# Windowed attention with sink tokens, then a gated two-layer MLP, on one core: a searched order of work written out, with another load order and another first score stage

## The chip, the core and the metric

The kernel runs on one core of one Trainium2 chip. The metric is device microseconds (us) per execution. One launch takes the inputs from HBM and leaves the output in HBM.

The engines are TensorE (PE: matmuls and transposes), VectorE (DVE), ScalarE (ACT: exp, tanh, copies), GpSimd (POOL) and SyncE (SP: issues most DMAs). DMAs can also be issued by ACT and by POOL; each issuing engine has a queue of its own.

## The reference

```python
# q, k, v: (4 batches, 8 heads, 768 positions, 64)
scores = q @ k.T / 8                        # per batch and head
keep = (key < 4) | (0 <= query - key < 128) # 4 sink keys, window of 128
a = softmax(where(keep, scores, -1e9))
x = (a @ v) as (4*768 tokens, 8*64 features)
h = x @ w_in                                # 512 -> 2048
out = (h * sigmoid(beta * h)) @ w_out       # 2048 -> 512
```

## The kernel before, in words

**Tiling.** The 3072 tokens are cut into 8 half batches (hb 0 to 7) of 384 tokens. A *unit* u is a pair of heads in one half batch, so there are 32 units, four to a half batch. PE does six kinds of step, and their names are used in this document:

- T(u): transposes q and k of a unit on PE (line 725, six matmuls), then two copies PSUM to SBUF (`qkT`). From half batch 3 on, DMA transposes do this instead.
- S(n): a *burst* of score tiles, matmuls of 64 rows (line 823). ACT takes the exp of each tile into a slot of `E` (line 840), and DVE or POOL multiply the masks in (lines 848, 854, 858). A tile is 128x1024: four 128x128 blocks of two heads each; `s` blocks touch the sinks, `d` blocks the diagonal, `p` blocks the block left of it.
- F: sink scores of a half batch against the four sink keys (line 870), exp into `ES` (line 874).
- A(u): attention times values (lines 915 and 926), then on DVE a reciprocal (line 930) and a product into `onorm` (line 932).
- R(u): transposes `onorm` on PE (line 952) and copies it into `xT`; from half batch 3 on by DMA.
- H(T, m): one of 16 column blocks of the first MLP layer for half batch T: four matmuls (line 970), tanh on ACT (line 975), product on DVE into `g` (line 977).
- O(T, t, j): four of the 16 matmuls of an output tile (line 993); the last is followed by a copy to `osb` and a store.

H and O carry most of PE's work: 128 H and 100 O.

**Order.** Nothing is ordered at run time. A planner in the kernel's own Python (class Graph) gives each operation an estimated duration. PE's steps of the first part are written by hand (the string in line 1188 and the list `early` in line 1228); later ones are taken by the loop in line 1260, which asks of each kind when it could start (`head`). `arrange` then re-sorts all engines with one constant for a hand-over between engines (HOP, line 35) and may move a PE step past up to ten others (WIDE, SKIP). PSUM has eight banks; `choose` picks the one free first. `any_of` lets several engines compete for a copy, a cast or a mask. While PE would wait in the first part, the planner inserts matmuls on a tile of ones (line 1212, "fill").

**Loads.** Before: SP issues q of half batch 0 in four pieces of 192 KB, its v in three pieces of 256 KB (rows of 256 B), q and k of half batch 1 (768 KB each), beta, then the weight pieces w0 to w15 (512 KB each; line 616). ACT issues the four pieces of k of half batch 0. Weights go through six staging buffers; w6 waits until w0 is cast, and so on. Values of the sink tokens (`vS`) for batch 0 come from a matmul with a selection matrix (`first_values_pe`, line 676): PE line 680, then DVE line 682.

Of the kernel before, what the change touches and what calls it, by code (L numbers as in the profile page):

```python
# [7 lines left out]
ALU = mybir.AluOpType  # L8
# [14 lines left out]
class Op:  # L23
    __slots__ = ("eng", "fn", "deps", "signal", "count", "waits", "sem", "vc", "dma", "seq", "end", "ns", "alts",
                 "group", "tail", "hold", "lock", "chain", "preds", "ready", "left", "succ", "at")


class Graph:
# [6 lines left out]
    HOP = 180  # L35
    SKIP = 3
    PAD = 100
    STRICT = 1
    WIDE, EARLY = 10, 60000
    SLACK = 0  # L40
# [3 lines left out]
    def __init__(self):  # L44
        self.ops = []
        self.writers = {}
        self.readers = {}
        self.last_x = {}
        self.free = {e: 800.0 for e in self.ENGINES}
        self.dma_free = 2500.0  # L50
        self.stalls = [(16000.0, 1100.0), (34000.0, 700.0)]
        self.port = {"gp": 0.0, "dve": 0.0}
        self.group = 0
        self.filler, self.fill_to = None, 0

# [4 lines left out]
    def add(self, eng, fn, ns=0, r=(), w=(), x=(), dma=None, alts=None, after=(), hold=550, chain=None, lock=False):  # L60
# [9 lines left out]
        o.lock = lock  # L70
# [22 lines left out]
        for p, _ in deps:  # L93
            at = max(at, p.end + (0 if p.eng == eng and not p.dma else self.HOP))
# [4 lines left out]
    def fill(self, fn, r):  # L99

        def one():
            o = Op()
            wide = self.free["pe"] + 2 * self.filler[0] <= self.fill_by
            o.eng, o.fn, o.dma, o.ns = "pe", fn[wide], None, self.filler[0] * (1 + wide)
            o.signal, o.count, o.waits, o.vc, o.lock = False, 0, [], None, False
            o.deps = [(p, True) for k in r for p in self.writers[k]]
            return o
        self.filler, self.fill_to = (self.COLD, one), self.group

    def shut(self, o, eng):  # L110

        return self.port["gp" if eng == "dve" else "dve"] if eng == "gp" or eng == "dve" and o.lock else 0.0

    def place(self, o, at):
# [3 lines left out]
        if o.dma:  # L118
# [4 lines left out]
            o.end = self.dma_free + 1000  # L123
        else:
            o.end = self.free[o.eng] = at + o.ns

    def at(self, keys):

        t = 0.0
        for k in keys:  # L130
            ws = self.writers.get(k)
            if not ws:
                return None
            t = max([t] + [p.end + self.HOP for p in ws])
        return t

    def bank_at(self, k):
        return max([0.0] + [p.end + self.HOP for p in self.last_x.get(k, ())])

    def arrange(self):  # L140
# [10 lines left out]
        follow, last = {}, None  # L151
        for o in ops:
            if o.chain is not None:
                if last is not None:
                    follow[id(last)] = o
                    o.left += 1
                last = o
        after = None
        for o in reversed(ops):
            o.tail = max([s.tail + self.HOP for s in o.succ] + [0.0])  # L160
# [3 lines left out]
            o.tail += o.ns + (2000 if o.dma else 0)  # L164
        groups = {}
        for o in ops:
            if o.eng == "pe":
                groups.setdefault(o.group, []).append(o)
        todo_pe = list(groups.values())
        self.free = {e: 800.0 for e in self.ENGINES}  # L170
        self.dma_free = 2500.0
        self.stalls = [(16000.0, 1100.0), (34000.0, 700.0)]
        self.port = {"gp": 0.0, "dve": 0.0}
        new, planned = [], set()

        def ready(o, e):
            return max([0.0] + [p.end + (0 if p.eng == e and not p.dma else self.HOP) for p in o.preds])

        def done(o):
            planned.add(id(o))  # L180
            new.append(o)
            for s in o.succ:
                s.left -= 1
                if s.left == 0 and s.eng != "pe":
                    pool.append(s)
            if id(o) in follow:
                s = follow[id(o)]
                s.left -= 1
                if s.left == 0:
                    pool.append(s)  # L190

        pool = [o for o in ops if o.left == 0 and o.eng != "pe"]
        while todo_pe or pool:
            best = None
            wide = self.SKIP if self.free["pe"] > self.EARLY else self.WIDE
            if todo_pe and todo_pe[0][0].group <= self.fill_to:
                wide = self.STRICT
            for i, grp in enumerate(todo_pe[:wide]):
                own = set(map(id, grp))
                if any(id(p) not in planned and id(p) not in own for o in grp for p in o.preds):  # L200
                    continue
                t, off = self.free["pe"], 0.0
                for o in grp:
                    t = max([t] + [p.end + self.HOP - off for p in o.preds if id(p) not in own and p.eng != "pe"])
                    off += o.ns
                if best is None or t < best[0] - self.SLACK:
                    best = (t, "pe", i)
                if t <= self.free["pe"]:
                    break
            by_eng = {}  # L210
            for o in pool:
                opts = []
                for e, (fn, ns) in o.alts.items():
                    t = max(self.free[e], ready(o, e), self.shut(o, e))
                    if o.dma:
                        t = max(t, self.dma_free - 3000)
                    opts.append((t + ns, t, e))
                _, t, e = min(opts)
                by_eng.setdefault(e, []).append((t, o))
            first = {}  # L220
            for e, c in by_eng.items():
                t0 = min(c, key=lambda x: x[0])[0]
                first[e] = (t0, max((x for x in c if x[0] <= t0), key=lambda x: x[1].tail)[1])
# [4 lines left out]
            for e, (t0, o) in first.items():  # L228
# [4 lines left out]
            if e == "pe":  # L233
                grp = todo_pe.pop(what)
                late = t + self.PAD if t > self.free["pe"] + 40 else t
                self.fill_by = late
                while self.filler and grp[0].group <= self.fill_to and self.free["pe"] + self.filler[0] <= late:
                    o = self.filler[1]()
                    self.place(o, max([self.free["pe"]] + [p.end + self.HOP for p, _ in o.deps]))
# [5 lines left out]
                for o in grp:  # L245
                    self.place(o, max([self.free["pe"]] + [p.end + self.HOP for p in o.preds if p.eng != "pe"]))
# [149 lines left out]
def _program(nc, G, sb, ps, q, k, v, w_in, w_out, beta, out):  # L396
# [4 lines left out]
    CUT = 3  # L401
# [25 lines left out]
    sel = sb("sel", (128, 128), BF16)  # L427
# [16 lines left out]
    WIDE_W, SPL, BQ = 2, ('act','gp'), "sp"  # L444
    EARLY, BST, SOON = 0, [1,2,2]+[3]*5, 2200
    LANES, QUADS = [6,7], [5,7]
    P = ps("P", (128, 8, 512))

    def add(eng, fn, ns, r=(), w=(), x=(), dma=None, after=(), hold=550, chain=None):
        return G.add(eng, fn, ns, r, w, x, dma, None, after, hold, chain)  # L450

    def any_of(alts, r=(), w=(), x=(), lock=False):

        return G.add(min(alts, key=lambda e: G.free[e] + alts[e][1]), None, 0, r, w, x, None, alts, lock=lock)
# [22 lines left out]
    held, reserve = {7}, [False]  # L477
    ring, two = [[6,5,4]], [[0,1],[2,3],[0,1],[2,3],[4,5]]

    def choose(n):  # L480

        if n == 1:
            runs = [[j] for j in (LANES if reserve[0] else range(8)) if j not in held]
            return min([(max(G.bank_at(("B", j)) for j in c), c[0] not in LANES, c) for c in runs], default=None)
        runs = [[]]
        for _ in range(n // 2):
            runs = [r + [i, i + 1] for r in runs for i in range(r[-1] + 1 if r else 0, 7, 2) if not held & {i, i + 1}]
        return min([(max(G.bank_at(("B", j)) for j in c), c[0] in LANES, c) for c in runs], default=None)

    def banks_at(n, more=False):  # L490
        c = choose(n)
        if c and more:
            rest = [G.bank_at(("B", j)) for j in range(8) if j not in held and j not in c[2]]
            return max(c[0], min(rest)) if rest else None
        return c and c[0]

    forced = []

    def take(n):
        if forced:  # L500
            got = [forced.pop(0) for _ in range(n)]
        elif ring[0]:
            if n == 1:
                got = ring[0].pop(0)
                ring[0].append(got)
                got = [got]
            else:
                got = list(range(n))
                if n == 2:
                    got = two.pop(0)  # L510
        else:
            got = choose(n)[2]
# [20 lines left out]
    def consts():  # L533
# [5 lines left out]
        add("gp", lambda e: e.memset(sel[:, :], 0.0), 80, w=["sel0"])  # L539
        add("gp", lambda e: e.tensor_copy(  # L540
            sel[:, :].rearrange("p (h w) -> p h w", w=16)[:, :, 0:NSINK],
            ident[:, 0:NSINK].unsqueeze(1).to_broadcast([128, H, NSINK])), 150, r=["sel0", "ident"], w=["sel"])
# [47 lines left out]
    def load(hb, n, i):  # L590

        b, t0, z = hb // 2, hb % 2 * HALF, hb % NSTG
        if n == "v" or hb >= CUT:
            src = {"q": q, "k": k, "v": v}[n][b, :, t0 + i * 128:t0 + (i + 1) * 128, :].rearrange("h p d -> p h d")
            dst, keys, ns = stg[n][z][:, i, :, :], [("stb", n, z, i)], NV0 if hb < 2 else 1092
        else:
# [4 lines left out]
            ns = NQ0 * len(keys) if hb == 0 else 1950 if hb == 1 else 2080  # L601
            keys = [("stg", n, z, j) for j in keys]
        after = [("stg", n, z, j) for j in range(4)] if hb in range(CUT, CUT + NSTG) and n != "v" else ()
        add("act" if hb == 0 and n == "k" and Q2 else "sp", lambda e: e.dma_start(dst, src), ns, w=keys,
            dma=f"d{n}{z}{'' if i is None else i}", after=after, chain=hb if hb < 3 else None)

    def load_w(j):
# [721 lines left out]
```

## Time and profile before

| what | value |
|---|---|
| three timed runs | 221.11, 222.12, 222.97 us (median 222.12) |
| profiled execution: its own time, first to last instruction | 219.7 us |
| median of the runs less that span | 2.4 us |
| PE busy | 213.4 us, 97% |
| PE weight loads | 120.8 us, 55% |
| DVE / ACT / POOL busy | 138.1 / 147.2 / 75.2 us |
| granted TensorE clock, mean | 1.000 |
| fill matmuls on ones | 35, 11.3 us busy |
| moved by DMA | 39.86 MB |

The profiled execution is one execution apart from the timed runs. A busy engine is not one that advances the result: fill counts as busy. The chain of work that ended last is 38% line 993 and 36% line 970, both on PE.

### The profile page before, as it was taken

To read this page: it belongs to the slowest core of one execution; us is meant where nothing else is said; L and a number is where in the kernel's file an instruction comes from. 1 tells how busy PE (TensorE), PEld (TensorE's weight loads), DVE (VectorE), ACT (ScalarE), POOL (GpSimd) and SP (SyncE) were. 2 spreads that over 40 slices of the span, in tenths; PEclk is the share of its full clock that TensorE was granted. 3 is DMA by queue.
4 is the path that set the end of the run, shared out by engine and by line. 5 is a ranking of instruction groups with operands and counts; after the bars stand their busy time and mean duration, and the time that the engine had idled before them with its cause. 6 is when DMAs were issued, how large, how long until landed. Compare 5 with 4: busy or idle time off the path is not lost.

```text
span 219.7 us, 4563 instructions
## 1 busy us (share of the span) xinstructions
PE 213.4 (97%) x1776; PEld 120.8 (55%) x1793; DVE 138.1 (63%) x293; ACT 147.2 (67%) x241; POOL 75.2 (34%) x140
## 2 busy tenths in 40 slices
PE   8999999999999999999999999999999999999995
PEld 3455557555575575446554556446565456465443
DVE  1697899697774278358960788478886248088000
ACT  2698999586975798459865597275886574187211
POOL 7344551112550790067103770184101770100100
PEclk9999999999999999999999999999999999999999
DMA  6999999999989998499837997659949111400122
GB/s 190 240 302 364 357 287 357 371 298 204 226 185 188 225 141 217 92 253 218 196 74 180 228 182 203 139 142 237 136 98 209 40 63 27 144 2 0 51 95 95
DMA packets 94717, 39.86 MB, mean 181 GB/s; under 512 B 82072, under 2 KB 89512, under 8 KB 94696
## 3 DMA queue, kind: packets, MB, share of 16 engines
q1 hardware_dynamic: 91928, 33.28, 68.9%
q0 software_dynamic: 1680, 5.51, 7.5%
q10 hardware_dynamic: 1088, 0.79, 1.1%
q8 instruction: 14, 0.23, 0.5%
q14 instruction: 7, 0.06, 0.1%
HBM read 27.37 MB, written 6.29 MB: 153 GB/s over the span
## 4 chain that ended last, share of the span: by engine, by line
PE 88%; DVE 6%; DMA 3%; ACT 2%; issue 1%; ACTq 0%
PE P L993 38%; PE P L970 36%; PE P L926 5%; PE P L823 4%; DMA k_stage<-in_k_dram 3%; DVE E L858 2%; PE P L725 2%; PE P L952 1%; DVE g L977 1%; PE P L915 1%; DVE E L848 1%; PE P L870 1%; PE P L1212 1%; DVE w_in L528 1%; ACT E L840 0%
## 5 line engine op out<-in xcount | busy, mean ns | idle before, releaser
L970 PE MATMUL P<-xT,w_in 128*128 128x384 bf16 x512 | 86.8, 327 | 0.4 <-ACT w_in L523 0.2
L993 PE MATMUL P<-w_out,g 128*128 128x512 bf16 (+2 forms) x383 | 84.6, 371 | 1.0 <-issue 0.2
L975 ACT ACTIVATE t<-P,hbeta 128x384 f32<-128x384 f32 x128 | 72.4, 590 | 17.6 <-PE P L970 11.0
L977 DVE SCALAR_TENSOR_TENSOR g<-t,P 128x384 bf16<-128x384 f32 x128 | 67.9, 550 | 21.1 <-ACT t L975 15.7
L970 PEld LDWEIGHTS P<-xT,w_in 128*128 128x128 bf16 x512 | 49.0, 98 | 33.4 <-DVE g L977 0.8
L993 PEld LDWEIGHTS P<-w_out,g 128*128 128x128 bf16 x400 | 37.3, 98 | 40.5 <-issue 0.5
L840 ACT ACTIVATE E<-P 128x1024 bf16<-128x1024 f32 x44 | 43.1, 1036 | 14.1 <-PE P L823 14.1
L854 POOL TENSOR_SCALAR_AFFINE_SELECT E<-E 128x512 bf16<-128x512 bf16 x59 | 38.8, 684 | 27.4 <-ACT E L840 27.2
L1011 POOL DMA_DIRECT2D out_dram<-osb x21 | 11.8, 562 | 63.5 <-ACT osb L523 63.5
L523 ACT ACTIVATE osb<-P 128x512 f32<-128x512 f32 x14 | 8.4, 597 | 25.1 <-PE P L993 25.0
L932 DVE TENSOR_TENSOR onorm<-P,rden 128x384 bf16<-128x384 f32 x32 | 17.6, 554 | 0.8
L529 DVE TENSOR_SCALAR osb<-P 128x512 f32<-128x512 f32 x9 | 6.2, 688 | 15.0 <-PE P L993 14.9
L848 DVE TENSOR_TENSOR E<-E,maskS 128x512 bf16<-128x512 bf16 x16 | 8.8, 564 | 10.4 <-ACT E L840 10.4
L926 PE MATMUL P<-vaug,E 128*128 128x65 bf16 x352 | 15.0, 193 | 0.0
L926 PEld LDWEIGHTS P<-vaug,E 128*128 128x128 bf16 x352 | 14.0, 97 | 1.4 <-ACT E L840 0.4
L823 PEld LDWEIGHTS P<-qkT 64*128 64x128 bf16 x288 | 9.5, 94 | 7.6 <-issue 4.3
L823 PE MATMUL P<-qkT 64*128 64x128 bf16 (+1 forms) x288 | 13.2, 230 | 0.1
L1212 PE MATMUL P<-ones 128*128 128x512 bf16 (+1 forms) x35 | 11.3, 446 | 1.1 <-POOL ones L534 1.1
L528 DVE CAST vaug<-v_stage 128x512 bf16<-128x512 f32 x19 | 9.5, 509 | 3.2 <-DMA v_stage<-in_v_dram 3.1
L697 POOL TENSOR_TENSOR kS<-qkT,headm 128x8 bf16<-128x8 bf16 (+1 forms) x10 | 2.5, 251 | 17.7 <-DMA qkT<-k 9.5
L915 PE MATMUL P<-vS,ES 128*128 128x130 bf16 x40 | 8.1, 221 | 0.4 <-DVE vS L682 0.4
L525 POOL TENSOR_SCALAR_AFFINE_SELECT q<-q_stage 128x512 bf16<-128x512 f32 x7 | 4.8, 693 | 10.4 <-DMA q_stage<-in_q_dram 10.4
(64 smaller groups left out, 119.6 us busy)
## 6 DMA issues: line engine op xcount, KB each, us to landing
v_stage<-in_v_dram SPq DMA_DIRECT2D x24, 256.0 KB, 4.8
out_dram<-osb POOLq DMA_DIRECT2D x21, 256.0 KB, 3.6
q_stage<-in_q_dram SPq DMA_DIRECT2D x15, 256.0 KB, 4.8
k_stage<-in_k_dram SPq DMA_DIRECT2D x15, 256.0 KB, 4.9
wst<-in_moe_w_in_dram SPq DMA_DIRECT2D x5, 512.0 KB, 8.3
wst<-in_moe_w_out_dram SPq DMA_DIRECT2D x4, 512.0 KB, 8.1
g<-in_moe_w_out_dram SPq DMA_DIRECT2D x4, 512.0 KB, 6.6
q_stage<-in_q_dram SPq DMA_DIRECT2D x2, 768.0 KB, 7.8
```

Of the source, the lines that this page charges most:

```text
L528: return lambda e: e.tensor_copy(dst, src)
L823: add("pe", lambda e, dst=dst, kt=kt, kc=kc, rows=rows, q0=q0, nq=nq, u=u: e.matmul(dst, kt[rows, kc:kc + 128], qkT[rows, u % NT, 0, q0:q0 ...
L840: add("act", lambda e, src=src, dst_=dst_: e.activation(dst_, src, AF.Exp, bias=0.0, scale=SCALE), act_ns(1024), w=[("E", z)] + [("m", z, ...
L854: alts = {"gp": (lambda e, dd=dd, sg=sg: e.affine_select(dd, dd, [[0, 4], [sg, 128]], ALU.is_ge, 0.0, base=min(sg, 0), channel_multiplier= ...
L926: e.matmul(A[:, c0:c0 + D + 1], E[t_ % NE][:, i, hh, :], vaug[vz][:, kb % NK, 2 * hp + hh, :], start=a, stop=o, skip_group_check=True), 31,
L932: add("dve", lambda e: e.tensor_tensor(onorm[on][:, :, :, :].rearrange("p m h d -> p (m h) d"), av[:, :, 0:D], rden[on][:, :].unsqueeze(2) ...
L970: add("pe", lambda e, c=c: e.matmul(hp, w_in16[:, c, m * 128:(m + 1) * 128], xT[:, c, t0:t0 + HALF], start=(c == 0), stop=(c == 3)), mm_ns ...
L975: add("act", lambda e: e.activation(tt[ti][:, :], hp, AF.Tanh, bias=0.0, scale=hbeta[:, m:m + 1]), act_ns(HALF) + 93, r=["hbeta"], w=[("t" ...
L977: add("dve", lambda e: e.scalar_tensor_tensor(gt[T_ % NG][:, m, :], tt[ti][:, :], 1.0, hp, ALU.add, ALU.mult), dve_ns(HALF), r=[("t", ti)] ...
L993: add("pe", lambda e, m=m: e.matmul(P[:, bk, 0:n], gt[T_ % NG][:, m, t * 128:(t + 1) * 128], w_out16[:, m, cols], start=(m == 0), stop=(m ...
L1011: add(eng, lambda e: e.dma_start(out_t[3 * T_ + t], osb[z][:, :]), 262144 / 300, r=[("osb", z)], dma=f"do{eng}{z}", hold={"sp": 550, "gp": ...
L1212: G.fill([lambda e, n=n: e.matmul(P[:, 7, 0:128 * n].rearrange("p (a b) -> p a b", a=n), ones[:, :], ones[:, :].unsqueeze(1).to_broadcast( ...
```

## The change

1. **Order written out.** The string ORDER lists every PE step with its PSUM banks, `LOADING` every early load with its queue, `KNOBS` the engine and an earliest planned time for single copies, casts and masks. `head`, `choose`, the planning loop and the re-sorting of PE are gone; PE now runs its steps strictly as listed.
2. **The planner's numbers.** Hand-overs have a time per pair of engines, loads share bandwidth, a queue holds a limited number of rows, and a list of times at which all loads stop for a while (`STALLS`) is counted in. These change only what order the other engines get.
3. **Loads.** SP: sink values, q piece 3, k piece 0, q piece 2, all of k of half batch 1, v pieces 0 and 1, beta, v piece 2, w0, w1, w3, w2, w5, w4, w6, ... ACT: k piece 3, q pieces 0 and 1, k pieces 1 and 2, all of q of half batch 1.
4. **First scores.** In half batch 0 the one `p` tile of four units becomes two half tiles (128x512) of two units, each a burst of its own; so hb 0 has bursts S0 to S5 instead of S0 to S4, and all later bursts are numbered one higher. F of half batches 0 and 1 are steps of their own.
5. **Sink values of batch 0** come from a load of 32 KB at the head of SP's queue; the selection matrix and its matmul are gone.

Core of the diff:

```diff
-    HOP = 180
+    HOPS = {("act", "dve"): 145, ("act", "pe"): 172, ("act", "gp"): 185, ("dve", "pe"): 147, ...
+    STALLS = [(7500.0, 650.0), (17800.0, 1250.0), (36000.0, 500.0), (41000.0, 800.0)]
...
-            for i, grp in enumerate(todo_pe[:wide]):
+            if nxt < len(todo_pe) and not open_[todo_pe[nxt][0].group]:
+                best = (starts(todo_pe[nxt]), "pe", None)
...
+        if hb == 0:
+            out_ = []
+            for i in range(4):
+                out_.append([("s", i, 0, 0), ("s", i, 0, 1), ("d", i, 1, 1), ("d", i, 2, 2)])
+                if i % 2:
+                    out_.append([("p", i - 1, 1, 2), ("p", i, 1, 2)])
+            return out_
...
-    def first_values_pe():
-        add("pe", lambda e: e.matmul(P[:, bk[0], :], sel[:, :], vaug[0][:, 0, :, 0:D], start=True, stop=True), mm_ns(512),
-    for x in "T0:63 T1:01 S1:01 T2:64 T3:46 S0:12 S4:56 S3:34 S2:01 F:2 V:5 A1:1 A0:5 A2:4 R0:5 A3:2 R1:0 R2:4 R3:0".split():
-    early = "H0 T4 H1 H2 H3 T5 H4 T6 T7 H5 S5 H6 H7 H8 H9 S6 H10 H11 S7 H12 H13 H14".split()
+    LOADING = "f q0.3 k0.0 k0.3@a q0.2 k1 v0.0 v0.1 q0.0@a b v0.2 w0 q0.1@a w1 k0.1@a k0.2@a w3 w2 w5 q1@a w4 w6 v1.2 w7 v1.1 v1.0 w8 w9 w10 w11 w13 w14 w15 w12"
+    ORDER = "T3:35 S4:56 T0:55 T1:00 T2:46 S0:23 S2:01 S1:45 S3:23 F0:1 S5:23 T6:43 T4:61 T7:33 B:4 A0:5 A2:6 T5:32 A1:4 A3:5 R0:1 R2:6 Z R1:3 S6:4501 R3:7 H:3 H:7 S7:4501 F1:6 H:2 H:3 H:5 H:4 H:2 H:0 H:7 H:6 H:3 S8:1245 H:0 H:7 H:2 H:3 H:6 A5:4 A6:7 A4:1 A7:2 O:5 O:4 O:6 R4:0 ...
```

In ORDER the digits behind a colon are banks, B is the transpose of beta, Z ends the fill.

More of the change, by code (lines that the diff above doesn't have):

```diff
@@ L93, in add @@
         for p, _ in deps:
-            at = max(at, p.end + (0 if p.eng == eng and not p.dma else self.HOP))
+            at = max(at, p.end + self.hop(p, eng))
         self.place(o, at)
@@ L117, in place @@
             self.port[o.eng] = at + (o.hold if o.dma else o.ns)
-        if o.dma:
+        if o.due:
+            o.at = max(at, o.due[0])
+            self.free[o.eng] = max(at, o.due[1])
+            o.end = o.landed + self.LAG
+        elif o.dma and o.parts:
+            ring = self.rings.setdefault(o.eng, [])[-9:]
+            out = at + o.hold
+            for i in range(len(ring)):
+                left = sum(x[1] for x in ring[i + 1:]) + o.parts
+                if left + ring[i][1] > self.RING:
+                    out = max(out, ring[i][0] - max(0.0, self.RING - left) / ring[i][1] * ring[i][2])
+            self.free[o.eng] = out
+            slow = o.chain is None
+            self.dma_free = max(self.dma_free, out + self.REACH) + o.ns * (self.LATER if slow else 1.0)
+            while self.stalls and self.dma_free > self.stalls[0][0]:
+                self.dma_free += self.stalls.pop(0)[1]
+            self.rings[o.eng].append((self.dma_free, o.parts, o.ns))
+            o.end = self.dma_free + self.LAG + (self.MARGIN if slow else 0.0)
+        elif o.dma:
             self.free[o.eng] = at + o.hold
@@ L122, in place @@
                 self.dma_free += self.stalls.pop(0)[1]
-            o.end = self.dma_free + 1000
+            o.end = self.dma_free + 1000 + (self.MARGIN if o.eng == "sp" else 0.0)
         else:
[L125 to L138, printed above, removed]
+            o.end = self.free[o.eng] = at + o.ns * (1.8 if o.eng == "pe" and o.group is not None and at < self.SLOW else 1.0)
     def arrange(self):
@@ L168, in arrange @@
                 groups.setdefault(o.group, []).append(o)
+                open_[o.group] = open_.get(o.group, 0) + sum(p.eng != "pe" or p.group != o.group for p in o.preds)
         todo_pe = list(groups.values())
         self.free = {e: 800.0 for e in self.ENGINES}
-        self.dma_free = 2500.0
-        self.stalls = [(16000.0, 1100.0), (34000.0, 700.0)]
+        self.dma_free, self.rings = 1950.0, {}
+        self.stalls = list(self.STALLS)
         self.port = {"gp": 0.0, "dve": 0.0}
-        new, planned = [], set()
+        first_loads = []
+        for o in ops:
+            if o.chain is not None:
+                if o.preds:
+                    break
+                first_loads.append(o)
+        self.loads(first_loads)
+        new = []
         def ready(o, e):
-            return max([0.0] + [p.end + (0 if p.eng == e and not p.dma else self.HOP) for p in o.preds])
+            return max([0.0] + [p.end + self.hop(p, e) for p in o.preds])
         def done(o):
-            planned.add(id(o))
             new.append(o)
@@ new lines, in done, with enter, starts @@
+                    enter(s)
+        def enter(o):
+            o.ready = {e: max(ready(o, e), o.early) for e in o.alts}
+            pool.append(o)
+        def starts(grp):
+            g = grp[0].group
+            if g not in due:
+                off, due[g] = 0.0, 0.0
+                for o in grp:
+                    due[g] = max([due[g]] + [p.end + self.hop(p, "pe") - off for p in o.preds if p.eng != "pe"])
+                    off += o.ns
+            return max(self.free["pe"], due[g])
@@ L474, in where @@
         return u // 8, u // 4 % 2, u % 4
[L477 to L497, printed above, removed]
-    def take(n):
[L500 to L512, printed above, removed]
+    held, forced = {7}, []
+    def take(n):
+        got = [forced.pop(0) for _ in range(n)]
+        assert not held & set(got)
         held.update(got)
@@ L710, in XP @@
             dma=f"x{n}{hb % 3}{c}", hold=1310)
-        for j in range(4):
-            mark(("qkTu", 4 * hb + j, i, c), ("qkT", z0 + j, i, c))
         if hb % 2 == 0 and (n, c) == ("k", 0):
@@ L779, in _program @@
                 LAST[b_[1]] = n_
-    def units_scored():
-        u = 0
-        while u < NU and LAST[u] < done["SC"]:
-            u += 1
-        return u
     def SC(n):
@@ L791, in SC @@
         bs = take(2 * len(tiles))
-        f_ = take(1) if first else None
+        f_ = take(1) if first is not None else None
         for j, t_ in enumerate(tiles):
@@ new lines, in beta_load @@
+    def beta_load(via):
+        add(via, lambda e: e.dma_start(beta_st[:, :], beta.rearrange("(m p) -> m p", p=128)), 20, w=["beta_st"],
+            dma="dbeta", chain=2, hold=500, parts=20)
+    consts()
+    for x in LOADING.split():
+        x, _, via = x.partition("@")
+        via = {"": "sp", "a": "act"}[via]
+        if x == "b":
+            beta_load(via)
+        elif x == "f":
+            load_first(0, via)
+            first_values(0)
+        elif x[0] == "w":
+            load_w(int(x[1:]), via)
+            cast_w(int(x[1:]))
+        else:
+            hb, _, i = x[1:].partition(".")
+            hb, n, i = int(hb), x[0], int(i) if i else None
+            load(hb, n, i, via)
+            for c in range(NK if i is None else 1):
+                cast(hb, n, c if i is None else i)
@@ L1111, in background @@
+    at = {"load": len(xl(0) + xl(1)) + 16, "cast": len(xl(0)) + (9 if len(xl(1)) == 5 else 11), "x": 0}
     def background():
-        now = G.free["pe"]
         moved = True
@@ L1155, in background @@
-            if n_w[0] < 16:
-                t = G.at([("win", n_w[0])])
-                if t is not None and t <= now + AHEAD:
-                    cast_w(n_w[0])
-                    n_w[0] += 1
-                    moved = True
-    for x in xl(0):
-        load(*x)
-        if x[1] == "v":
-            mark(("in",) + x, ("stb", "v", 0, x[2]))
-    for i in range(4):
-        for n in "qk":
-            mark(("in", 0, n, i), ("stg", n, 0, i))
-    consts()
-    done["load"] = 11
-    for u in range(4):
-        cast(0, "q", u)
-        cast(0, "k", u)
@@ new lines, in background @@
+            if at["x"] < len(XPS):
+                hb, n, c = XPS[at["x"]]
+                if at["cast"] > CASTS.index(XPS[at["x"]]) and done["T"] == 4 * hb and all(LAST[u] in seen for u in range(4 * (hb - NT // 4 + 2))):
+                    XP(hb, n, c)
+                    at["x"] += 1
+                    if at["x"] % 6 == 0:
+                        done["T"] += 4
+                        seen.update(("T", 4 * hb + j) for j in range(4))
+                    moved = True
+            i = done["R"]
@@ L1197, in _program @@
             bk = take(1)
-            SS(0, bk[0])
+            SS(i, bk[0])
             give(bk)
+            seen.add(("F", i))
         else:
-            step(x[0], int(x[1:]))
-    ring[0] = [6,0,1,2,3]
-    def beta_load():
-        add(BQ, lambda e: e.dma_start(beta_st[:, :], beta.rearrange("(m p) -> m p", p=128)), 20, w=["beta_st"],
-            dma="dbeta", chain=2 if BQ == "sp" else None)
-    for x in "".split():
-        x, _, bk = x.partition(":")
-        forced[:] = [int(c) for c in bk]
-        step(x[0], int(x[1:]))
@@ new lines, in _program @@
+            G.fill([lambda e, n=n: e.matmul(P[:, 7, 0:128 * n].rearrange("p (a b) -> p a b", a=n), ones[:, :],
+                                            ones[:, :].unsqueeze(1).to_broadcast([128, n, 128]), start=True, stop=True)
+                    for n in (2, 4)], ["ones"])
+            give([7])
+        if x in done:
+            done[x] += 1
+        assert not forced
+    background()
+    assert done["H"] == len(HS) and done["O"] == len(OS) and done["R"] == done["A"] == NU and done["S"] == len(BURSTS)
```

547 lines of the change are left out of this document (224 added, 323 removed).

## The prediction

> **What bounds the kernel now.** I read the busy times first, then the chain of work that ended last in order of time, then rates by microsecond for the loads, then what ACT and DVE do before the first MLP step.
>
> ```profile
> PE 213.4 (97%) x1776; PEld 120.8 (55%) x1793; DVE 138.1 (63%) x293; ACT 147.2 (67%) x241; POOL 75.2 (34%) x140
> PE   8999999999999999999999999999999999999995
> PEclk9999999999999999999999999999999999999999
> L1212 PE MATMUL P<-ones 128*128 128x512 bf16 (+1 forms) x35 | 11.3, 446 | 1.1 <-POOL ones L534 1.1
> ```
>
> PE is busy from end to end, but 11.3 us of it is fill, all before 19 us. So the question is where useful work becomes dense. The chain, in order of time:
>
> ```profile
> 17.11 0.34 PE P L952 x3
> ...
> 19.05 0.33 PE P L952 x3
> ...
> 20.02 0.49 ACT qkT L523
> 20.51 0.53 ACT w_in L523
> 21.03 0.14 issue
> 21.17 1.46 PE P L970 x8
> 22.63 0.34 PE P L725 x6
> ...
> 31.45 2.77 PE P L970 x16
> ```
>
> The first H starts at 21.17. From there to PE's last end at 217.29 are 196.1 us, in which waits add up to about 0.5 us at most. The middle of the run shows the same:
>
> ```profile
> 180.00:200.00 20.00, 19.95 (x162) 11.43 (x162) 11.99 (x26) 11.26 (x20) 1.13 (x3) 1.00 0.21 60
> ```
>
> (length, then busy time of PE, its weight loads, DVE, ACT, POOL, then granted clock, DMA share, GB/s.) PE is at 19.95 of 20. No reordering can shorten that stretch, since the matmuls are the same; it can only add waits. A gain must come from an earlier H0.
>
> **The change part by part.**
>
> *What H0 must do to be even.* In the changed list T7 (0.34, the row above) and a burst of scores (S5 before, 0.62 a burst, with 0.1 of switch) stand ahead of the first H instead of behind it. The dense stretch is therefore 1.06 us shorter: 195.0. H0 at 217.29 − 195.0 = 22.25 gives the old span; each microsecond later costs one.
>
> *When H0 can start: loads.* Windows of one microsecond, same columns, and the queues from 3 to 5 us:
>
> ```profile
> 3.00:4.00 1.00, 1.00 (x3) 0.30 (x2) 0.01 (x1) 0.00 (x0) 1.00 (x5) 1.00 1.08 352
> 11.00:12.00 1.00, 1.00 (x19) 0.66 (x20) 0.95 (x3) 0.99 (x2) 0.92 (x3) 1.00 0.63 132
> 13.00:14.00 1.00, 1.00 (x9) 0.38 (x6) 1.00 (x3) 1.00 (x2) 0.60 (x2) 1.00 1.07 360
> ```
> ```profile
> q1 hardware_dynamic: 487, 0.35, 54.4%
> q10 hardware_dynamic: 456, 0.33, 49.4%
> ```
>
> SP's queue (q1) and ACT's (q10) share evenly, and the two together move 352, as much as SP's alone at 13 us (360). So the second queue adds no pace.
>
> The last piece of half batch 0 is now k piece 2, fifth on ACT's queue. Call its landing L. Before, ACT's pieces (192 KB) landed at 4.29, 7.22, 8.46 and 9.19: 1.63 each, so a fifth would land at 10.6 at worst. At 352 a pair of pieces, one on each queue, takes 1.12, which gives 4.1 + 4 × 1.12 = 8.6 at best. I take the middle, 9.5: the slow v rows of 256 B, which ran beside the pieces before, now come later, but shares and pace are not fixed by a row.
>
> *From L to H0: ACT's queue.*
>
> ```profile
> 8.48 0.52 ACT L523 ACTIVATE k<-k_stage 128x384 bf16<-128x384 f32 x1 [0.64 <-DMA k_stage<-in_k_dram]
> 11.39 2.86 ACT L840 ACTIVATE E<-P 128x1024 bf16<-128x1024 f32 x3
> 18.39 0.86 ACT L523 ACTIVATE xT<-P 128x384 bf16<-128x384 bf16 x2
> 30.15 2.06 ACT L975 ACTIVATE t<-P,hbeta 128x384 f32<-128x384 f32 x4
> ```
>
> Back to back, ACT needs some 0.93 for an exp of 128x1024, 0.38 for a copy into qkT (like xT: two in 0.86), 0.45 for a cast and 0.5 for a tanh. The half tile (128x512) has no row. It lies between 0.49 (128x384, the sink exp) and 1.02 (a full tile); I take 0.48, nearest to the size, and 0.5 more for each of two is its upper end. In ACT's new order after L: the cast, four copies (L+2.0), then three full exps, two half ones, casts of q and k of half batch 1 and of v, the sink exp, and the copy of T6: about L+8.1. PE takes its steps as listed; T7's bank 3 is T6's, so T7, the beta transpose and A0 stand behind that copy: A0 at L+8.7. This is the wait that the change adds; all four A, R and H0 are queued behind it.
>
> After A0 the DVE row decides:
>
> ```profile
> 15.50 0.18 DVE L930 RECIPROCAL rden<-P 128x6 f32<-128x6 f32 x1
> 18.35 0.56 DVE L932 TENSOR_TENSOR onorm<-P,rden 128x384 bf16<-128x384 f32 x1
> ```
>
> Reciprocal and product of four units took from 15.50 to 18.91, 0.75 a unit with what lies between. So the last onorm ends at L+12.2. S6 stands ahead of R3, so R3 is ready at L+12.75 and the copy of its xT (0.49) lets H0's fourth matmul go at L+13.4. The first three can run before it: H0 effectively at L+12.9 = 22.4. With full durations in place of start-to-start times the chain is 0.9 longer, 23.3. I take **22.8**: 0.55 later than even. With L from 8.6 to 10.6 the bounds are 21.5 and 24.4.
>
> *The other road to H0: v piece 2.* A0 needs it too. By then 3.96 MB must have moved. Before, that total stood at 16.3, with a gap of 0.6 at 11 to 12 us (132 in the row above, as SP issued late), so 15.7 without it; a landing followed its total by 1.3 (q of half batch 1: 13.9, 15.19). So it lands at 17.0, the POOL cast takes 0.66, and A0 goes at 17.7, against L+8.7 = 18.2 by ACT. H0 would follow at 21.9. The two roads are close; ACT's is the later. Weight w0 landed at 19.10 before and has over 2 us.
>
> *Edits at nothing.* The selection matrix (0.20 and 0.21 on POOL), its matmul (0.39) and the DVE op (0.68) go; a masked op of 0.7 to 1.1 comes on DVE at about 5.5, where DVE was 0.43 busy and then 0.00 in the next microsecond. Were it late, F0 has until A0. The 32 KB load costs SP one issue, 0.46, ahead of q piece 3; L is set by ACT's queue, otherwise 0.46. One burst more costs a switch of 0.19 in idle PE time, at most 0.19 of the end. ACT issues six loads, done at 4.4, before its first copy (5.9); past that each would be 0.5 to 1 on its chain. Fill is about as much as before.
>
> *The end of the fill.* The first ten fill matmuls took 4.45 (0.44 each; 0.27 later), though the clock row shows 1.00 throughout; nothing in this trace shows a slow pace coming back, and the gaps of up to 0.4 us between transposes and A steps at 17 to 21 us left H0 at its full pace (8 in 1.46). I cost it at nothing, 223.0; rival C has the other case. The Trainium skill, page "TensorE: Matmul & The Clock Gate", Part 1 ("The HAM clock gate"), says that an idle window of about 3.4 us halves PE's clock until a busy window has passed; if PE's pieces of idleness after Z counted as such a window, the sum by this rule would be near C's time. The trace bears out its start (0.44), and no run shown here its return.
>
> *After H0.* In the new list A24 has four matmuls of an O step (0.86) and twelve of H (12 × 0.163 = 1.95, from 6.50 for 40 in the chain) after its last burst: 2.8 of cover where about 3.5 stood. Exp and mask of the last tile need about 3.0: +0.2 (0 to 0.5). Bank hand-overs in the written list: +0.1 (0 to 0.5).
>
> *Sum.* 0.55 + 0.2 + 0.1 = +0.9: span 220.6. The median of the runs was 2.4 above the profiled span (219.7, 222.12): **223.0 us**.
>
> **The rivals.**
>
> *A, faster.* ACT has slack because casts slip between exps, and L comes at 8.6; then H0 is set by v piece 2: 21.9, or 21.2 if that lands at 16.3. With no later waits the span moves by 21.55 − 22.25 = −0.7 at the middle of the two: 221.4. For it: the gap of 0.6 in the loads goes. Against: five of ACT's pieces in a row must land at the full pace, which 267 and 236 GB/s at 5 and 8 us did not show. The H run cannot be much earlier, since w7 landed at 30.71 and its cast takes 0.69; if loads all run at 352 it goes further, past −2.2.
>
> *B, slower: ACT sets the H run.* From the fifth exp to the 15th tanh ACT has 14.7 us of work by its back-to-back times, where PE has 12.3. If the first tanh starts more than 1.2 us later than I have it, H steps wait for banks and the run ends 2.5 later: 225.5. For it: 12 qkT copies are on ACT instead of 8. Against: before, ACT waited for PE at 22.02.
>
> *C, the pace of PE falls again.* Fill ends at Z, and PE idles in pieces from 19 to 22.8. If the pace of the first matmuls returned for their 4.4 us, half of it, 2.2, would be lost: 225.2. For it: the changed kernel has less to do on PE there. Against: R and T steps and a burst still fall into it.
>
> *D, many small waits.* The written order was laid out for estimated durations; each of 128 H and 100 O that comes 10 ns late for its bank costs 2.3 in all: 225.3 and above. Against: 19.95 of 20.
>
> **How the numbers follow.** Chances: forecast 0.44 (its own range 221.8 to 224.3), A 0.26, B 0.15, C 0.06, D 0.09. One per cent, about what a measurement of this kernel tells from no change, is 2.2 us. Of A 0.12 lies beyond it (loads at full pace throughout), the other 0.14 within; B, C and D lie beyond it: faster 0.12, same 0.44 + 0.14 = 0.58, slower 0.30. The range leaves out about 0.12 of A below 220.0 and 0.08 of B to D above 225.9.
>
> **What would show it.** The start of the first matmul of the H line against 22.25 and 22.8; ACT unbroken from the cast of k piece 2 to the copy of T6, and A0 right behind that; v piece 2 landing near 17.0. Rival A shows as A0 waiting for v, B as H matmuls released by tanh, C as H matmuls of 0.3 instead of 0.16 apart, D as waits spread over the H and O lines. I am wrong if PE has gaps beyond 0.5 us after H0, or if H0 starts before 21.5 or after 24.4.

## The result, and the profile after

Over 20 runs each: the changed kernel 224.08 us (222.05 to 226.1), the kernel before 221.69 (221.11 to 223.1). Ratio 1.0087, 95% interval 1.0068 to 1.0105; that is 1.9 us. One disturbed run of the changed kernel (226.1) is left out of the ratio; the medians with it would give 1.0108. The profiled execution took 223.62 with a span of 221.9, 2.2 more than the span before.

The page of the changed kernel has the same shape (columns as before):

```profile
PE 215.1 (97%) x1796; PEld 121.5 (55%) x1796; DVE 132.5 (60%) x291; ACT 150.5 (68%) x250; POOL 73.9 (33%) x132
PEclk9799999999999999999999999999999999999999
```

PE's busy time rose by 1.7 us. That is less than it looks: 0.9 of it is fill (12.2 against 11.3), and the trace of before lacks the records of 17 of the 400 matmuls of the O steps (its page has x383). The second slice of the clock row is new. The timeline of PE shows where it bites. In the changed kernel fill is line 1185, T is line 766, S 863, A 956 and 967, R 993, H 1011 and O 1034.

```profile
6.97 0.34 PE L766 MATMUL P<-ident,q 128*128 128x128 bf16 x3 [1.70 <-DVE q L583]
...
8.62 2.10 PE L1185 MATMUL P<-ones 128*128 128x512 bf16 x5
10.51 0.53 PE L766 MATMUL P<-ident,q 128*128 128x128 bf16 x3
...
23.98 1.60 PE L1011 MATMUL P<-xT,w_in 128*128 128x384 bf16 x8
```

PE stood idle for 1.70 us before its first transposes at 6.97. Then transposes took 0.53 instead of 0.34, and five fill matmuls 2.10. Before, the first transposes came at 5.31, and the second group had its full pace:

```profile
5.31 0.53 PE L725 MATMUL P<-ident,q 128*128 128x128 bf16 x3
...
6.99 0.33 PE L725 MATMUL P<-ident,q 128*128 128x128 bf16 x3
```

The windows of one microsecond (granted clock third from the right) name the reason:

```profile
7.00:8.00 1.00, 1.00 (x9) 0.51 (x9) 1.00 (x3) 0.65 (x2) 0.00 (x0) 1.00 1.08 350
8.00:9.00 1.00, 0.85 (x8) 0.34 (x8) 0.82 (x3) 0.91 (x3) 0.20 (x1) 0.76 1.11 342
10.00:11.00 1.00, 1.00 (x8) 0.66 (x7) 0.54 (x2) 0.16 (x1) 0.00 (x0) 0.50 1.10 327
12.00:13.00 1.00, 1.00 (x15) 0.57 (x13) 0.96 (x2) 0.87 (x3) 0.23 (x2) 1.00 1.20 287
```

The clock fell to 0.50 at about 8.5, 1.5 us after the idle time had ended, and was back by 12 us. And the idle time comes from SP's queue:

```profile
0.80 0.79 SPq L716 DMA_DIRECT2D vS<-in_v_dram  x1
1.65 0.42 SPq L655 DMA_DIRECT2D q_stage<-in_q_dram  x1
```

The 32 KB load held SP for 0.79, q piece 3 was issued at 1.65 and landed at 6.46; before, the first piece was issued at 0.81 and landed at 3.96:

```profile
0.81 2.00 SPq L604 DMA_DIRECT2D q_stage<-in_q_dram  x4
```

The first H moved from 21.17 to 23.98. From there to PE's last end (219.40) are 195.4 us, with one wait that the trace names; before, 196.1:

```profile
PE P L956 <- DVE g L1018: 0.6, 1, 0.6
```

So in this execution the late first H explains most of the loss: it came 1.7 after the 22.25 at which it would have been even, and PE's last end moved by 2.15. The rest lies in the stretch, which has the wait of 0.6.

### The profile page after: what moved, and what is told of

Same layout as the page of the kernel before. It is cut to its first block, busy times and chain, and to the rows that moved or that the text cites. A ratio compares the mean times of both kernels' runs of the same rounds, so it can differ in the third digit from the quotient of the medians.

```text
span 221.9 us, 4554 instructions
## 1 busy us (share of the span) xinstructions
PE 215.1 (97%) x1796; PEld 121.5 (55%) x1796; DVE 132.5 (60%) x291; ACT 150.5 (68%) x250; POOL 73.9 (33%) x132
## 4 chain that ended last, share of the span: by engine, by line
PE 85%; DVE 8%; ACT 3%; DMA 2%; SPq 0%; issue 0%
PE P L1034 38%; PE P L1011 33%; PE P L863 4%; PE P L967 4%; DVE g L1018 3%; ACT E L881 2%; DMA q_stage<-in_q_dram 2%; DVE E L899 2%; PE P L766 2%; PE P L1185 1%; DVE onorm L973 1%; PE P L956 1%; DVE w_in L583 1%; ACT qkT L578 1%; PE P L993 1%; PE P L911 1%
## 5 line engine op out<-in xcount | busy, mean ns | idle before, releaser
L1034 PE MATMUL P<-w_out,g 128*128 128x512 bf16 (+2 forms) x400 | 91.9, 371 | 0.0
L1011 PE MATMUL P<-xT,w_in 128*128 128x384 bf16 x512 | 91.7, 326 | 0.0
L881 ACT ACTIVATE E<-P 128x1024 bf16<-128x1024 f32 (+1 forms) x45 | 42.9, 1017 | 7.9 <-PE P L863 7.8
L578 ACT ACTIVATE osb<-P 128x512 f32<-128x512 f32 x17 | 10.2, 600 | 13.9 <-PE P L1034 13.9
L967 PE MATMUL P<-vaug,E 128*128 128x65 bf16 x352 | 16.2, 193 | 0.0
L889 DVE TENSOR_TENSOR E<-E,maskS 128x512 bf16<-128x512 bf16 x14 | 7.4, 537 | 10.1 <-ACT E L881 10.1
L1185 PE MATMUL P<-ones 128*128 128x512 bf16 (+1 forms) x39 | 12.2, 444 | 1.1 <-POOL ones L589 1.1
L578 ACT ACTIVATE qkT<-P 128x384 bf16<-128x384 bf16 (+1 forms) x15 | 7.6, 561 | 7.3 <-PE P L766 7.0
L583 DVE CAST vaug<-v_stage 128x512 bf16<-128x512 f32 x15 | 7.4, 491 | 8.3 <-DMA v_stage<-in_v_dram 8.2
L583 DVE CAST k<-k_stage 128x512 bf16<-128x512 f32 (+1 forms) x15 | 7.2, 497 | 3.6 <-DMA k_stage<-in_k_dram 3.6
L971 DVE RECIPROCAL rden<-P 128x6 f32<-128x6 f32 x32 | 5.8, 185 | 3.4 <-PE P L967 3.3
```

What stands on the lines that cost most here:

```text
L578: return lambda e: e.activation(dst, src, AF.Copy, bias=0.0, scale=scale)
L583: return lambda e: e.tensor_copy(dst, src)
L881: add("act", lambda e, src=src, dst_=dst_: e.activation(dst_, src, AF.Exp, bias=0.0, scale=SCALE), act_ns(256 * nb), w=[("E", z, e0 + i) f ...
L967: e.matmul(A[:, c0:c0 + D + 1], E[ZAT[t_][0]][:, i, hh, :], vaug[vz][:, kb % NK, 2 * hp + hh, :], start=a, stop=o, skip_group_check=True), 31,
L1011: add("pe", lambda e, c=c: e.matmul(hp, w_in16[:, c, m * 128:(m + 1) * 128], xT[:, c, t0:t0 + HALF], start=(c == 0), stop=(c == 3)), mm_ns ...
L1034: add("pe", lambda e, m=m: e.matmul(P[:, bk, 0:n], gt[T_ % NG][:, m, t * 128:(t + 1) * 128], w_out16[:, m, cols], start=(m == 0), stop=(m ...
```

## The experiments

The table is read with the texts below it. "Stretch" runs from the first H to PE's last end in the one profiled execution of each kernel; the ratio comes from repeated runs.

| kernel | first transposes | first H | last end | stretch | ratio to before |
|---|---|---|---|---|---|
| before | 5.31 | 21.17 | 217.25 | 196.1 | 1 |
| changed | 6.97 | 23.98 | 219.40 | 195.4 | 1.0087 (1.0068 to 1.0105) |
| small load late | 5.09 | 22.41 | 221.16 | 198.8 | 1.0068 (1.0035 to 1.0102) |
| more fill | 6.12 | 22.84 | 220.77 | 197.9 | 1.0109 (1.0075 to 1.0143) |
| A4 before A6 | 6.68 | 22.38 | 219.84 | 197.5 | 1.0101 (1.0056 to 1.0146) |
| before + small load | 6.46 | 22.82 | 219.80 | 197.0 | 1.0064 (1.0035 to 1.0092) |
| half later loads | 6.81 | 24.89 | 220.52 | 195.6 | 1.0075 (1.0044 to 1.0106) |
| first H held | 6.87 | 25.65 | 220.51 | 194.9 | 1.0145 (1.0103 to 1.0186) |
| one p tile | 6.38 | 23.40 | 221.97 | 198.6 | 1.0127 (1.0078 to 1.0176) |
| before, w0 first | 5.30 | 20.70 | 217.65 | 197.0 | 1.0001 (0.9976 to 1.0026) |
| small load late, half later loads | 5.09 | 22.31 | 218.19 | 195.9 | 1.0057 (1.0023 to 1.0091) |
| small load late, sinks early | 5.04 | 23.82 | 221.24 | 197.4 | 1.0105 (1.0073 to 1.0137) |
| before, half later loads | 5.31 | 20.69 | 217.29 | 196.6 | 0.9975 (0.9945 to 1.0006) |

The profiled execution with the small load late took 225.38, 2.0 above the median of that kernel's runs, so its stretch is too long to be typical. Each stretch is a single execution: before, its w0-first variant and its control with half the loads differ by 0.9.

**Small load late.** Edit on the finished order: on SP's queue

```
-vS  q3  k0  q2  k(hb 1) ...
+q3  k0  q2  vS  k(hb 1) ...
```

and the DVE product that uses it behind the first two masks.

> The changed kernel, with its 32 KB load issued as fourth on SP's queue instead of first, and the DVE product that uses it moved behind the first masks; nothing else moves. Theory L (the small load at the head holds back the first pair, PE idles for 1.7 us, its clock falls and the first transposes are slow): q piece 3 lands near 5 instead of 6.46, the granted clock stays 1.00, the first exp after k piece 2 starts near 12.0 instead of 13.16, the first H near 22.8 instead of 23.98; about 1.2 us less than the changed kernel, ratio to before 1.003. Rival K (k piece 2 and ACT's queue alone set the first H): first H within 0.3 of 23.98, ratio 1.008.

The first H came as theory L said, and PE no longer idles or slows:

```profile
5.09 0.37 PE L766 MATMUL P<-ident,q 128*128 128x128 bf16 x3
...
7.94 0.34 PE L766 MATMUL P<-ident,q 128*128 128x128 bf16 x3
```

The time did not follow by 1.2 us: 1.0068 is the lower end of the changed kernel's interval, and L's 1.003 lies just outside this run's own interval. In the profiled execution, what the first H won came back as waits of PE (the one for `vS` is 0.4 in the run with A4 ahead of A6, so its 1.1 here is not typical):

```profile
PE P L956 <- DVE vS L722: 1.1, 1, 1.1
PE P L956 <- DVE g L1018: 0.6, 1, 0.6
PE P L993 <- DVE onorm L973: 0.4, 1, 0.4
```

**Before + small load.** Edit: `+dma_start(vS32, v[0, :, 0:16, :])` at the head of SP's queue.

> The kernel before with a 32 KB load of the sink values put at the head of SP's queue and not used (the matmul with the selection matrix stays). Theory L: the first piece of q lands 0.8 to 1.5 us later than 3.96, the first transposes start after 6 instead of 5.31, the first H 0.5 to 1.2 later; ratio 1.002 to 1.005. Rival K: the delay is hidden before the first exps, ratio within 0.001 of 1.

Measured 1.0064, more than the 1.002 to 1.005 expected, and by the expected way: the first piece landed at 5.96 instead of 3.96, the first transposes came 1.15 later, the second group was still at half pace (0.53; before, 0.33), and the first H came 1.65 later.

```profile
6.46 0.50 PE L725 MATMUL P<-ident,q 128*128 128x128 bf16 x3 [0.95 <-DVE q L528]
8.58 0.53 PE L725 MATMUL P<-ident,q 128*128 128x128 bf16 x3
10.70 0.34 PE L725 MATMUL P<-ident,q 128*128 128x128 bf16 x3
```

This load alone, at the head of the queue, costs the kernel before some 1.4 us (0.0064 of 221.5). In the profiled execution PE also waited 1.4 us for a product of an H step at 33 us, and its last end came 2.55 later than before; at 224.04 it is 1.0 above the median of these runs.

**More fill.** `+5 x matmul(ones, 512)` behind the first ten.

> The changed kernel with five more 512-wide fill matmuls at the start (15 instead of 10), so that PE does not idle before the first transposes; loads as they are. Theory C (the clock that falls after the idle time costs the 1.6 us between k piece 2 and the first exp after it): no granted clock below 1.00, transposes of 0.33 instead of 0.53, first H near 22.8, ratio to before about 1.003. Rival (the clock is not what counts, since most timed runs of the changed kernel show a mean of 1.000 and are as slow): ratio 1.008 to 1.009.

All transposes took 0.34, no granted clock was below 1.00, and the first H came at 22.84, as theory C said of the early part. The ratio did not fall, so the rival was right on the time. Again the stretch is longer, with waits on casts of weights and on a DMA transpose:

```profile
PE P L1011 <- POOL w_in L580: 0.7, 1, 0.7
PE P L1011 <- DMA xT<-onorm: 0.6, 1, 0.6
PE P L1034 <- DVE w_out L583: 0.4, 1, 0.4
```

**A4 before A6.** `-A5:4 A6:7 A4:1 A7:2` `+A5:4 A4:1 A6:7 A7:2`

> The changed kernel with A4 (bank 1) ahead of A6 (bank 7) in the list. Theory B (the wait of 0.61 us at 37 us is a bank handed over late by an H step's product): the wait goes or shrinks to under 0.2, 0.4 to 0.6 us less than the changed kernel, ratio to before 1.006. Rival (the product is late for the next user of a bank too): the wait moves to the third A step, ratio 1.008 to 1.009.

The wait for that bank went, as B had it, and others came, so the time is nearer the rival's. By chance the clock did not fall in this profiled execution, although the first transposes were nearly as late:

```profile
6.68 0.34 PE L766 MATMUL P<-ident,q 128*128 128x128 bf16 x3 [1.39 <-DVE q L583]
...
8.32 1.15 PE L1185 MATMUL P<-ones 128*128 128x512 bf16 x5
```

The same five fill matmuls took 1.15 instead of 2.10, and the first H came at 22.38. So the late first piece alone does not move the first H; the pace of PE behind it does. The execution also shows what the changed kernel does with an early first H:

```profile
PE P L863 <- DMA qkT<-k: 0.6, 1, 0.6
PE P L1034 <- ACT w_out L578: 0.5, 1, 0.5
PE P L956 <- DVE vS L722: 0.4, 1, 0.4
```

Three different engines are named, but DMA transposes, sink values and weights all come through SP's queue. That is theory F. The three waits add up to 1.5 us; the stretch is 2.1 longer than the changed kernel's, so part of it has no named wait.

**First H held.** In the list `R3:7 H:3` becomes `R3:7 X:2 H:3`, X being eight matmuls on ones.

> The changed kernel with eight matmuls on ones (8 x 0.216 = 1.7 us, of which about 0.4 lie in idle time) put between the last transpose into xT and the first H; they hold back the first H by about 1.3 us and change nothing else. Theory F (the end is set by deliveries after 30 us, an early H0 only waits later): at most 0.4 us more than the changed kernel, ratio to before 1.008 to 1.011, dense stretch near 196. Rival (PE is dense from the first H on, as the prediction had it): 1.3 us more, ratio 1.014 to 1.016.

1.0145: the rival's number, and F's 1.008 to 1.011 is missed. A first H held back from the changed kernel's costs most of what it is held: in the profiled executions 1.67 later at the first H are 1.11 at the last end, and the ratios differ by 1.3 us. The stretch of 194.9 is the shortest of all, with a wait of 0.4 for `vS` in it; the prediction's 195.0 for the dense stretch was right. So deliveries do not set the end whatever the first H is; F can hold only for an early one.

**Half later loads; small load late, half later loads; before, half later loads.** `+src, dst = src[:, 0:4], dst[:, 0:4]` for half batches 2 to 7.

> The changed kernel with the loads of q, k and v from half batch 2 on cut to half the heads (so the later scores and values are partly computed from old data); order, casts and number of DMAs stay. In the kernel with A4 and A6 exchanged the first H came at 22.38, as wanted, but the 197.5 us from there to the end hold some 2 us of waits for casts of weights, DMA transposes and sink values. Theory F (the list is ahead of what SP's queue of loads delivers after 30 us): the waits from 50 us on go, dense stretch 195.5 to 196.3, ratio to before 0.998 to 1.002. Rival G (the waits are between engines, not loads): ratio 1.007 to 1.010.

> The changed kernel with both edits: the small load fourth on SP's queue (as in the run with the small load late), and the loads of q, k and v from half batch 2 on cut to half the heads (part of the later result is computed from old data). The first H then comes near 22.4 and the question is what stands behind it. Theory F (what comes through SP's queue is late for an early first H): no wait for casts of q, k, v, for DMA transposes or sink values over 0.2 us after 50 us; dense stretch at most 196.3 instead of 198.8; ratio to before 1.001 to 1.004. Rival G (engines among themselves): dense stretch 197 and more, ratio 1.006 to 1.009.

> The kernel before with the loads of q, k and v from half batch 2 on cut to half the heads (control: part of the later result is computed from old data). It has no wait for a delivery to lose: by both theories the ratio is 0.998 to 1.001. If it is faster by more, the loads also slow other work, and the half loads of the other runs have to be read against this.

The first had G's ratio (1.0075; F had 0.998 to 1.002). It does not decide, since in its profiled execution PE was at half pace until about 13 us and the first H at 24.89, too late to show waits. With the small load late as well, the first H is at 22.31 and the stretch 195.9 instead of 197.5 to 198.8. The trace names only this:

```profile
PE P L1034 <- issue: 0.8, 5, 0.2
PE P L956 <- DVE g L1018: 0.6, 1, 0.6
PE P L1011 <- DVE g L1018: 0.2, 1, 0.2
```

The first row is no wait: this trace lacks 22 of the 400 matmuls of the O steps, which leaves gaps. The wait of 0.6 is the one for a bank at 36 us. No cast, transpose or sink value is late any more, and the stretch is within F's 196.3: in this one trace theory F holds. The timed runs give it no support. The ratio of 1.0057 is above what F had (1.001 to 1.004) and just below G's lowest (1.006), its interval holds both, and the gain on the run with the small load late, 0.0011, is less than the 0.0025 that the same cut gave the kernel before, which is itself not clear of nothing. Why this kernel is still half a per cent slower than before stays open.

**One p tile.** The line of tiles of half batch 0 back to `[("p", i, 1, 2) for i in range(4)]`, bursts renumbered.

> The changed kernel with the one p tile of four units (128x1024, burst S4) in half batch 0 again in place of two half tiles; load order and the later list stay, DVE and ACT get slightly other orders. The prediction costed the half tiles at the work they replace (2 x 0.48 against 0.93 on ACT): first H within 0.3 of the 22.4 of the run with A4 and A6 exchanged, ratio 1.007 to 1.011. Rival: the half tiles bring A0 and A1 forward, without them the first H comes 0.5 to 1 later; ratio 1.010 to 1.014.

The first H came at 23.40, 1.0 later than 22.38, and the ratio is in the rival's range, though the intervals overlap. But the cause is not the half tiles: the second group of transposes already starts 1.0 later (10.50 against 9.50), and so do the exp behind the copies (12.54 against 11.55) and A0 (19.18 against 18.16). The first transposes and the fill behind them were at half pace here (0.50, and 1.71 for five fill matmuls). From that exp to A0 both kernels take 6.6, so in these traces the half tiles cost what they replace, as the prediction had it. PE also waited 1.6 us for a DMA transpose later, the longest wait behind the first H in any run.

**Before, w0 first.** In ACT's order the cast of half of w0 changes places with the copy before it.

> The kernel before with ACT's half of the cast of w0 moved ahead of the copy of qkT that stands before it (20.02 and 20.51 in its chain); nothing else moves. Theory D0 (the kernel before is dense from its first H on and its first H waits for that cast): the first H at 20.65 instead of 21.17, 0.3 to 0.5 us less, ratio 0.998. Rival F (deliveries set the pace there too): the gain comes back as waits near w7 at 31 us, ratio 0.9995 to 1.0005.

The first H came 0.47 sooner and the end did not. The rival was right: PE waits 0.2 for the next weights, 0.2 for a product of an H step and 0.3 for a cast of k, none of which the trace of before has.

**Small load late, sinks early.** All three orders: the first small load fourth, A4 ahead of A6, later `vS` loads six places up SP's queue.

> The changed kernel with three edits of order: the first small load fourth on SP's queue, A4 ahead of A6, and the small loads of sink values of batches 2 and 3 six places earlier on SP's queue, ahead of the DMA transposes into xT. Nothing is left out. Theory F: the wait for sink values at 150 us (0.4 to 1.2 us) and that for a bank at 35 us (0.8) go, dense stretch near 196.8, ratio 1.002 to 1.004. Rival: other waits take their place, ratio 1.006 and more.

The waits for the bank and the sink values went, and PE waited 1.1 us for a DMA transpose instead; no gain. The first H was late here, at 23.82, for two reasons: k piece 2 landed at 10.49, and the clock fell here too, to 0.50 from about 11.5 to 15 us, although the small load was not at the head, the first transposes came at 5.04, and no idle stretch of PE near it was over 0.7 us. So the small load is not the only way to a fallen clock. With a first H this late the stretch was still 197.4. None of these kernels is clearly faster than the kernel before.

## Why the prediction was right, and where it was not

The forecast, 223.0 and slower by under 1%, had the sign and the class; the measured 224.08 lies inside its own range, near the upper end. The rise was mis-sized: 0.9 forecast, 1.9 measured by the ratio. The forecast is as near as it is partly because the 2.4 added to the span came from three runs; over 20 runs of the kernel before it is 2.0. Point by point, in the profiled execution:

- *Loads to L.* L was put at 9.5 and came at 9.49. v piece 2 was put at 17.0 and came at 17.18. Right.
- *The small load.* Costed at one issue of 0.46 that L hides. It took 0.79, and the first q came at 6.46. This is the step that failed: the price was sought at the last piece, and it lay at the first, where PE had nothing else to do. It is not the lateness itself that costs (first transposes at 6.68 and a first H at 22.38 go together in the run with A4 ahead of A6), but the half pace that can follow the idle time.
- *L to the first exp after it.* Put at 2.0, measured 3.7 (13.16): the clock had fallen. Of that, 0.95 went into five fill matmuls (2.10 instead of 1.15) that stand in the list ahead of the transposes; the prediction gave fill no price there. From there to A0 6.6 (put at 6.7), from A0 to the fourth matmul of H0 4.8 (put at 4.7). The rest of the chain held.
- *The clock (rival C).* Its mechanism happened, but in front of the transposes at 8 to 12 us and not behind Z, and its price was about 1.6 us of the chain, not 2.2 at the end. The Trainium skill, page "TensorE: Matmul & The Clock Gate", Part 1 ("The HAM clock gate"), has the fall after an idle window of about 3.4 us; here 1.7 us of idleness went ahead of it, and the lower clock lasted some 3.4 us. Here half of such a window of idleness was enough, and the measurement decides. The words of the Trainium skill there, that the window runs freely, fit the run with A4 ahead of A6, which idled nearly as long at 5.3 to 6.7 and kept its clock.
- *"Each microsecond later costs one", and A24 +0.2, banks +0.1.* Right in the executions of the changed kernel and of the held one, whose first H is at about 24 or later. For an earlier one it failed: at 22.3 to 22.8, in the runs with full loads, the stretch was 197.5 and more, not 195.3. The +0.3 for waits stood for what measured 2 us or more in those executions. The line is not sharp: a first H at 23.82 went with 197.4 in the last run. Rival D was nearer there, but with other waits than it had: most of those named are for deliveries, not for the written banks.
- *Its own signs.* The first H, 23.98, is inside 21.5 to 24.4. Two signs failed: ACT was to work without a break from the cast of k piece 2 on and idled 1.24 before 11.40, and the wait of 0.6 at 37 us is beyond the 0.5 allowed.
- *Slips in the sum.* 217.29 − 195.0 is 22.29, not 22.25, which is 0.04; a fifth piece 1.63 after 9.19 would land at 10.8, not 10.6, and the middle of the two bounds for L would be 9.7 instead of the 9.5 taken.

So two errors take each other's place: with a fallen clock the first H is late and PE waits for little, and with a full clock (A4 before A6) the first H is even 0.4 before the forecast and PE waits 2 us more than allowed. Either way the last end comes 2 to 2.6 us after that of the kernel before, more than twice the forecast rise, so that the number lies in its range at all owes something to luck. How often each of them occurs in the timed runs is open. The four runs whose mean clock records the fall (0.992) average 223.9 us, the other fifteen in the ratio 223.7, so the recorded fall by itself does not set the time. But in the kernel with half the later loads the transposes took 0.53 while the row said 1.00, so the mean doesn't count every slow start. That SP's queue, and not only how the list leans on it, makes the deliveries late was tried by less data alone; moving the DMA transposes to another queue was not tried.

## What to carry to other kernels

Price a load at the head of a queue by what its first consumer waits for, not by the last piece of the stage. Fill that stands ahead of useful work in the list becomes a cost when PE is slow. An earlier start of a dense stretch can be given back as waits inside it: read the waits in a run in which the start is early, since a late start hides them, and let repeated runs decide, which here they did not. One profile shows one execution: some 1.4 to 1.7 us of idle time at the same place were followed here by full pace, by a clock that fell later, and by half pace that lasted to 13 us.

## What the runs showed of the hardware

- In the kernel before, a single 32 KB load ahead of it moved the landing of the first 192 KB piece from 3.96 to 5.96, 2.0 us for 0.85 of later issue. In the changed kernel, where other loads moved too, it was 6.46.
- Half-pace matmuls appear with a clock row of 1.00 at the start of every kernel here (ten fill matmuls in 4.0 to 4.45). Where PE idled early they can last on: after 0.95 us of idleness to about 10 us (before + small load), after 1.51 to 13 us (half later loads); after 1.39 (A4 before A6) there were none.
- In the three executions whose clock fell after the start (changed, first H held, small load late with sinks early), PE had been busy for 1.56, 1.67 and 1.70 us of the 3.4 us before the fall, and the clock was back 3.4 us later. In the last of them the idleness came in pieces of at most 0.7 us.
